# A second Strassen level for one more product of a GEGLU's gate and up stage

## The chip, the cores and the metric

The kernel runs on one core of one Trainium2 chip. The metric is the device time of one execution in microseconds (us); lower is better. A core has TensorE (PE, matrix products into eight PSUM banks), VectorE (DVE), ScalarE (ACT), GpSimd (POOL) and SyncE (SP). The last two serve here mainly to issue DMAs: SP loads from DRAM, POOL stores, loads from buffers in DRAM and DMAs that add onto what is there. Each engine runs its own instructions in program order and waits on semaphores for the others.

## The reference

```python
g = sigmoid((x * gate_w).sum(-1, keepdims=True))
a = dft_seq_re @ (x @ dft_hid_re.T) - dft_seq_im @ (x @ dft_hid_im.T)
b = (gelu(x @ w_gate) * (x @ w_up)) @ w_down
return g * a + (1 - g) * b
```

`x` is 2048 x 640 (S x D), `w_gate` and `w_up` 640 x 1728 and `w_down` 1728 x 640, all in float32; gelu is the tanh form.

## The kernel before

Each float32 factor is held as two parts, a high one in the reduced type fp32r and a low one, the rest. A block product is three matmuls of 128x128 by 128x512 (`mm3`, high x high, high x low, low x high), accumulated in a PSUM bank of 128x512. `high` is a copy by ScalarE that rounds. The low part is made in two ways: `low` is a subtraction by VectorE; `negative` with `left_of` is ScalarE's copy of the raw value with the sign turned, and then an accumulating DMA on POOL's queue that adds to it.

The work runs in stages: the first chunk of gate and up, with x loaded and split (to about 45 us); gate and up for f = 1 to 12, chunks of 128 columns of `w_gate` and of `w_up` (to 337); the product with `w_down` (to 508); the DFT over the sequence; the DFT over the hidden axis, and the mix. All of the stages use Strassen's scheme in the Winograd form, with seven products of half size instead of eight, whose sums and differences VectorE makes.

In gate and up a chunk f is a 2x2 system: the left factors are blocks A11, A12, A21, A22 of the weights and their sums S1 to S4, the right factors B11 to B22 of x and T1 to T4, for each of two halves of the tokens (`tp` 0 and 1). A block is two block products long (index i), and a fifth row block, `g5` and `u5`, goes with it. `gate_up(f, ..., tp, ...)` is a generator that issues these products; at each `yield` the caller decides what comes next. Its banks are X (`pX`) and Z (`pZ`).

`pair_of(f)` gives the kind of a chunk. f = 1 and 2 are kind 0, each by itself. From f = 3 (`PAIRED`) chunks go in pairs, (3,4) to (11,12), the first of a pair of kind 1, the second of kind 2. Over a pair (two chunks) and the two halves of the tokens, the product A12 B21 is a 2x2 system of its own, and `together` computes it with a second Strassen level in seven block products instead of eight, with banks H, Z and V (`pH5t`, ...). Its left factors (`wq`) come from `make_w`, its right factors from `sums_across`, whose parts are kept in DRAM and loaded for each pair anew by `load_across` on POOL's queue (tiles `xq`). Its results are the tiles `s1`, to which the two `gate_up` of each chunk add.

SBUF tiles of 4 KB a partition come from a ring of 47 (`slot`, tag `s4`), tiles of 128x512 from a ring of 12 (`mtile`). A new tile waits until all that read or wrote the tile that had its place are done, DMAs among them.

The order on PE, ScalarE, VectorE and POOL is the order of the program text (`in_order`). Work for coming chunks lies in a queue `fills` of (cost, function) and is taken out in order by `fill` as PE's work goes on, in proportion to `pe_all`. In a chunk this holds: the sums left from the chunk before (`todo`), the left factors of f + 1 (`make_w`), the sums of `w_down` (`sum_wd`) and the totals for the gate g (`load_z`: a load of 128x640, `xz`, by SP, and a product and total by VectorE). In kind 1 these z totals are spread over the queue, three a chunk (four in the last). The results h and their differences are stored to DRAM (`keep`, tiles `hA` and `hT`).

Of the kernel before, what the change touches and what calls it, by code (L numbers as in the profile page):

```python
# [33 lines left out]
def kernel(  # L34
# [93 lines left out]
    wsd = [dram.tile([P, 8, P], F32, tag=f"wsd{k}", name=f"wsd{k}") for k in range(NK)]  # L128
    acc4 = dram.tile([P, 2, T], F32, tag="acc4", name="acc4")
# [21 lines left out]
    def load_x(tp):  # L151


        n = f"{tp}"
        B, r = {}, {}
        src = xt[2 * tp : 2 * tp + 2]

        def tiles(t):
            for k in (1, 2):
                r[k, t] = pair(F32, f"xr{n}{k}{t}")  # L160
                B[k, t] = hl(f"x{n}{k}{t}")
            if t == 1:
# [12 lines left out]
        def tsum(i):  # L175

            a, b = {1: ((1, 2), (1, 1)), 2: ((2, 2), "T1"), 3: ((2, 2), (1, 2)), 4: ((2, 1), "T2")}[i]
            r[f"T{i}"] = pair(F32, f"xs{n}{i}")
            tt(r[f"T{i}"], r[a], r[b], op=ALU.subtract)
            B[f"T{i}"] = hl(f"xT{n}{i}")  # L180

        def his(*keys):
# [22 lines left out]
    def load_w(f):  # L205
# [8 lines left out]
        if pair_of(f) == 1:  # L214
            rq = slot(F32, [P, 8, P], f"wq{f}r")
            nc.sync.dma_start(rq[:, 0:3], wf[f, :, 0:3])
        wraw[f] = ra, rb, rq

    def make_w(f):
# [5 lines left out]
        g23, g5, g01, u23, u5 = ra[:, 0:2], ra[:, 2], ra[:, 3:5], ra[:, 5:7], ra[:, 7]  # L225
# [29 lines left out]
        def diff_here():  # L255
            tt(ra[:, 2], g5, u5, op=ALU.subtract)

        low_from = 2 if kind == 2 else 0

        def high_a():  # L260
            own["a"] = parts("wa")
            high(own["a"][0][:, low_from:], ra[:, low_from:])

        def neg_a():
            negative(own["a"][1][:, low_from:], ra[:, low_from:])

        def low_a():
            a = own["a"]
            left_of(a[1][:, low_from:], ra[:, low_from:])
            W["u5"] = at(a, 7)  # L270
            if kind == 2:
                W["D"] = at(a, 2)
            else:
                W["g5"] = at(a, 2)
            for i in range(2):
                W["A12", i], W["A11", i], W["A22", i] = at(a, i), at(a, 3 + i), at(a, 5 + i)
# [8 lines left out]
        def low_q():  # L285
            q = own["q"]
            left_of(q[1][:, 1:], rq[:, 1:])
# [8 lines left out]
        def neg_c():  # L296
            negative(own["c"][1], own["s"])

        def low_c():
            c = own["c"]  # L300
            left_of(c[1], own["s"])
# [4 lines left out]
        def parts_of(hi, neg, lo):  # L306
            return [(0, hi), (0, neg), (0, lo)]

        a, c = parts_of(high_a, neg_a, low_a), parts_of(high_c, neg_c, low_c)
        if kind == 1:  # L310
            q = parts_of(high_q, neg_q, low_q)
            work = [*a[:2], (84, across), a[2], (56, across2), *q[:2], (84, sums), q[2], (84, sums2), *c[:2], (56, diff), c[2]]
        elif kind == 2:
            work = [(28, diff_here), *a[:2], (84, sums), a[2], (84, sums2), *c]
        else:
            work = [*a[:2], (84, sums), a[2], (84, sums2), *c[:2], (56, diff), c[2]]
# [49 lines left out]
    def together(f, W, Tp, s1, xs):  # L366
# [7 lines left out]
        s1[0, 0] = copy(H, f"s1{f}00")  # L374
# [31 lines left out]
    def gate_up(f, W, B, tp, s5, s1t, xs):  # L406
# [17 lines left out]
        if not kind:  # L424
            s1 = copy(X, f"s1{n}")
# [5 lines left out]
        if not kind:  # L431
            V = bank(f"pV{n}")
            prod(V, "A12", (2, 1), True)
            mm3(V, W["g5"], x1, False, True)
            yield 204
            tt(s1, s1, V, op=ALU.add)
# [5 lines left out]
        if not kind:  # L442
            nc.scalar.activation(s1, s1, AF.Gelu_apprx_tanh)
# [20 lines left out]
        prod(X, "A22", "T4", False)  # L464
        mm3(X, W["u5"], x1, False, True)
        yield 204
        tt(s2, s2, s5, op=ALU.mult)  # L467
        keep(hA[tp][k], 1 + 2 * second, s2)
        tt(s1, s1, X, op=ALU.mult)
# [21 lines left out]
    def sums_left(r, a21, to):  # L491


        a11, a12, a22 = r[:, 0:2], r[:, 2:4], r[:, 6:8]
# [13 lines left out]
    def sum_wd(k):  # L508

        r, a21 = slot(F32, [P, 8, P], f"dr{k}"), wsmall(F32, f"da{k}")  # L510
        nc.sync.dma_start(r, wd[k, :, :8])
        nc.sync.dma_start(a21, wd[k, :, 8:])
        return sums_left(r, a21, wsd[k])

    def sum_wu(p):


        r, a21 = slot(F32, [P, 8, P], f"ur{p}"), wsmall(F32, f"ua{p}")
        nc.sync.dma_start(r, wu[p, :, :8])
        nc.sync.dma_start(a21, wu[p, :, 8:])  # L520
        yield
        if p > 1:
            for a, b in ((0, 2), (2, 4), (4, 5), (5, 8)):
                if p < 4 or a not in (0, 4):
                    nc.scalar.activation(r[:, a:b], r[:, a:b], AF.Copy, scale=-1.0)
            if p < 4:
                nc.scalar.activation(a21, a21, AF.Copy, scale=-1.0)
            nc.gpsimd.dma_start(wneg[p], r)
            yield
        for _, do in sums_left(r, a21, wsu[p]):  # L530
            do()
        yield

    def gate_rows():

        nc.scalar.activation(z, z, AF.Sigmoid)
# [304 lines left out]
    with in_order(ACT, DVE, PE):  # L841
        nc.scalar.activation(table, table, AF.Gelu_apprx_tanh)
        idle = bank("idle")
        for k in range(14):
            nc.tensor.matmul(idle[:, : T // 2], *ones, start=True, stop=True, skip_group_check=True)
# [78 lines left out]
    Tp, t_raw = {}, {}  # L924

    def sums_across():


        raw = {}

        def load(name, b, d):
            raw[name] = mtile(F32, f"xp{name}")
            nc.sync.dma_start(raw[name], xt[b, d])

        for name, b, d in (("11", 0, 2), ("12", 2, 2), ("22", 2, 3), ("21", 0, 3)):
            load(name, b, d)

        def sums():
            raw["t1"] = mtile(F32, "xpt1")
# [7 lines left out]
        def part(k, v, src):  # L947
            return lambda: split(*v, src) or Tp.update({f"T{k}": v})

        def part_out(k, v, src):  # L950
            def do():
                part(k, v, src)()
                for i, p in enumerate(v):
                    nc.gpsimd.dma_start(across_t[k][:, i], p.bitcast(F32))
# [3 lines left out]
        pairs = hl("xpT")  # L958
        Tp.update(B11=at(Bs[0][2, 1], 0), B21=at(Bs[0][2, 1], 1), B22=at(Bs[1][2, 1], 1))

        def part3():
            part_out(3, (mtile(F32R, "xp3h"), mtile(F32R, "xp3l")), raw["12"])()

        def part1():
            part_out(1, at(pairs, 0), raw["t1"])()

        work = [(138, sums), (69, part1), (138, sums2), (69, part_out(2, at(pairs, 1), raw["22"])), (69, part3)]
        return work, [(69, part(4, at(Bs[1][2, 1], 0), raw["21"]))]

    across_t = {k: dram.tile([P, 2, T], F32, tag=f"xp{k}", name=f"xp{k}") for k in (1, 2, 3)}  # L970

    def load_across(f):
        if pair_of(f) != 1 or f == PAIRED:
            return
        for k in (1, 2, 3):
            v = slot(F32R, [P, 2, T], f"xq{f}{k}")
            nc.gpsimd.dma_start(v, across_t[k])
            Tp[f"T{k}"] = v[:, 0], v[:, 1]
# [20 lines left out]
    s1t = {}  # L999
    with in_order(PE, ACT, DVE, POOL):  # L1000
        for f in range(1, NF):
            kind = pair_of(f)
            if f == PAIRED:
                fills.extend(t34)
            fills.extend(todo)
            todo.clear()
            if f == PAIRED - 1:
                t12, t34 = sums_across()
                fills.extend(t12)
            if f + 1 < NF:  # L1010
                nxt, work = make_w(f + 1)
                fills.extend(work)
            if f >= PAIRED and (kind == 1 or f == NF - 1):
                fills.extend(sum_wd((f - PAIRED + 1) // 2))
            if kind == 1:
                more, zs = list(fills), load_z(4 if f > NF - 3 else 3)
# [7 lines left out]
            state.update(pe=0, done=0, all=sum(c for c, _ in fills), pe_all=2450 if not kind else 2790 if kind == 1 else 2040)  # L1024
            s5 = pair(F32, f"s5{f}")
            xs = {}
            work = [gate_up(f, W, Bs[tp], tp, s5[:, tp], s1t, xs) for tp in range(2)]
            more = together(f, W, Tp, s1t, xs) if kind == 1 else iter(())
            for _ in range(4):
                run(more)  # L1030
            for step in range(8 if not kind else 7):
                for tp, w in enumerate(work):
                    run(w)
                    if (step, tp) in ((0, 1), (1, 0)):
                        run(more)
                        if step == 0:
                            run(more)
                if step == 5:
                    load_w(f + 2)
                if step == 4:  # L1040
                    load_across(f + 1)
                if f == NF - 1 and step > 4:
                    load_k(step - 4)
            while fills:
                fills.popleft()[1]()
            if f == NF - 1:
                gate_rows()
            W = nxt
        for _, do in todo:
            do()  # L1050
# [3 lines left out]
    for i in range(len(kseq)):  # L1054
# [14 lines left out]
        step_k(i)  # L1069

# [376 lines left out]
```

## Time and profile before

| | us |
|---|---|
| median of 3 runs | 1026.74 (1025.98 to 1027.36) |
| the profiled execution | 1025.88 |
| its span | 1024.1 |
| VectorE busy | 759.8 |
| ScalarE busy | 475.4 |
| gate and up, f = 5 and 6 (143.2 to 191.5) | 48.3 |

The profile's page gives for each engine the busy time, its share of the span and the number of instructions; the chain that ended last, followed back from the last instruction; and the costliest groups of instructions. The trace can be asked for a stretch of time (windows), for what an engine waited for (waits), for groups of instructions by line, and for DMAs. A row of a group reads: line, engine, operation, out<-in, partitions x elements and type, how many; then the busy time and the mean of one in ns; then the idle time ahead of it and what ended most of it. A DMA row reads: out<-in, the queue, how many, KB each, and the median us from issue to landing. Buffer numbers are left out of names, so `pX` is any chunk's X bank and `s` any result tile.

### The profile page before, as it was taken

Reading aid. Unit: us, or ns where it says so; the run is one execution under the profiler, and the core shown is the slowest. Engines: PE = TensorE matmul, PEld = TensorE weight load, DVE = VectorE, ACT = ScalarE, POOL = GpSimd, SP = SyncE. Lnnn points to the kernel's source line nnn. Section 1 sums busy time; section 2 is a strip of 40 time slices with the busy share of each in tenths; the row PEclk is TensorE's granted clock in tenths of the full one; section 3 lists DMA queues with packets and bytes.
Section 4 is the critical chain, followed back from the end, with each engine's and each line's share of the span. In section 5 each row is a group of like instructions: output and inputs, shape, how many; then the busy total and the mean of one; then the engine's idle time right before and its main releaser. Section 6 shows DMA issues by size and latency. Waiting matters only on the chain.

```text
span 1024.1 us, 13114 instructions
## 1 busy us (share of the span) xinstructions
PE 1019.9 (100%) x4525; PEld 844.5 (82%) x4525; DVE 759.8 (74%) x1067; ACT 475.4 (46%) x609; POOL 186.9 (18%) x317
## 2 busy tenths in 40 slices
PE   9999999999999999999999999999999999999998
PEld 7888888888888888888888888888888888888887
DVE  6966756556566959976898975888488869797794
ACT  5645435353443647555455443444344344355340
POOL 0122433332433200100011012102110200021121
PEclk9999999999999999999999999999999999999999
DMA  7566887979799988968766768657875877997855
GB/s 269 167 183 195 266 251 227 284 187 282 205 310 323 380 295 301 345 184 296 279 209 220 263 235 312 231 193 261 300 245 196 282 265 280 328 314 221 264 142 91
DMA packets 87140, 258.19 MB, mean 252 GB/s; under 512 B 11585, under 2 KB 20961, under 8 KB 87073
## 3 DMA queue, kind: packets, MB, share of 16 engines
q1 hardware_dynamic: 59440, 171.34, 48.9%
q0 software_dynamic: 27344, 85.82, 28.6%
q8 instruction: 35, 0.57, 0.2%
q14 instruction: 33, 0.26, 0.1%
q10 hardware_dynamic: 288, 0.20, 0.1%
HBM read 177.54 MB, written 65.55 MB: 237 GB/s over the span
## 4 chain that ended last, share of the span: by engine, by line
PE 99%; DMA 0%; SPq 0%; DVE 0%; ACT 0%; issue 0%
PE pX L99 8%; PE pX L98 8%; PE pX L97 8%; PE pZ L99 5%; PE pZ L98 5%; PE pZ L97 5%; PE pL L98 3%; PE pL L99 3%; PE pL L97 3%; PE pV L98 2%; PE pV L99 2%; PE pV L97 2%; PE pY L98 1%; PE pR L98 1%; PE pQ L98 1%; PE pY L99 1%
## 5 line engine op out<-in xcount | busy, mean ns | idle before, releaser
L78 ACT ACTIVATE ch<-csa 128x1024 fp32r<-128x1024 f32 x32 | 34.0, 1063 | 88.3 <-DVE csa L612 73.4
L81 DVE TENSOR_TENSOR cl<-cra,ch 128x1024 fp32r<-128x1024 f32 x32 | 39.1, 1223 | 29.9 <-ACT ch L78 14.6
L457 DVE TENSOR_TENSOR s<-s,pX 128x512 f32<-128x512 f32 x24 | 16.5, 687 | 56.1 <-PE pX L99 41.7
L78 ACT ACTIVATE ch<-cra 128x1024 fp32r<-128x1024 f32 x32 | 33.9, 1058 | 51.1 <-PE pL L98 25.3
L98 PE MATMUL pL<-cl,xah 128*128 128x512 f32 x128 | 49.8, 389 | 0.0
L99 PE MATMUL pL<-ch,xal 128*128 128x512 f32 x128 | 49.8, 389 | 0.0
L97 PE MATMUL pL<-ch,xah 128*128 128x512 f32 x128 | 49.3, 389 | 0.0
L441 ACT ACTIVATE s<-pZ 128x512 f32<-128x512 f32 x24 | 14.4, 598 | 69.1 <-PE pZ L99 47.5
L81 DVE TENSOR_TENSOR cl<-crb,ch 128x1024 fp32r<-128x1024 f32 x32 | 39.1, 1222 | 8.1 <-ACT ch L78 7.2
L78 ACT ACTIVATE ch<-crb 128x1024 fp32r<-128x1024 f32 x32 | 33.8, 1055 | 19.9 <-DVE cl L81 8.2
L81 DVE TENSOR_TENSOR cl<-csb,ch 128x1024 fp32r<-128x1024 f32 x32 | 39.2, 1225 | 4.0 <-ACT ch L78 2.3
L81 DVE TENSOR_TENSOR cl<-csa,ch 128x1024 fp32r<-128x1024 f32 x32 | 39.0, 1219 | 3.6 <-DMA wsu<-ur 3.6
L81 DVE TENSOR_TENSOR kl<-kw,kh 128x1024 fp32r<-128x1024 f32 (+1 forms) x26 | 31.4, 1209 | 13.3 <-ACT kh L78 13.3
L78 ACT ACTIVATE ch<-csb 128x1024 fp32r<-128x1024 f32 x32 | 34.0, 1063 | 10.5 <-DVE csb L615 7.0
L143 ACT ACTIVATE s<-pX 128x512 f32<-128x512 f32 x44 | 25.6, 595 | 24.2 <-PE pX L99 23.8
L746 POOL DMA_DIRECT2D out<-ks x12 | 6.5, 543 | 163.8 <-DVE ks L745 163.2
L1116 POOL DMA_DIRECT2D uA<-c x8 | 4.3, 544 | 166.8 <-DVE c L1204 166.6
L342 POOL DMA_DIRECT2D hA<-s x48 | 26.4, 549 | 34.7 <-DVE s L467 25.0
L342 POOL DMA_DIRECT2D hT<-s x48 | 26.1, 544 | 27.0 <-DMA hA<-s 7.2
L78 ACT ACTIVATE kh<-kw 128x1024 fp32r<-128x1024 f32 (+1 forms) x26 | 27.1, 1042 | 7.7 <-issue 3.5
L462 ACT ACTIVATE s<-s 128x512 f32<-128x512 f32 x24 | 14.9, 629 | 33.7 <-DVE s L461 33.7
L97 PEld LDWEIGHTS pL<-ch,xah 128*128 128x128 f32 x128 | 24.0, 188 | 5.0
(3680 smaller groups left out, 3445.6 us busy)
## 6 DMA issues: line engine op xcount, KB each, us to landing
cra<-in_ct SPq DMA_DIRECT2D x64, 512.0 KB, 4.1
crb<-in_ct SPq DMA_DIRECT2D x64, 512.0 KB, 5.0
hA<-s POOLq DMA_DIRECT2D x48, 256.0 KB, 6.4
hT<-s POOLq DMA_DIRECT2D x48, 256.0 KB, 6.1
kr<-hA SPq DMA_DIRECT2D x24, 512.0 KB, 8.3
kr<-hT SPq DMA_DIRECT2D x24, 512.0 KB, 6.8
ux<-uA SPq DMA_DIRECT2D x24, 512.0 KB, 6.1
ux<-uT SPq DMA_DIRECT2D x16, 512.0 KB, 6.5
```

What stands on the lines that cost most here:

```text
L78: nc.scalar.activation(hi, raw, AF.Copy)
L81: nc.vector.tensor_tensor(lo, raw, hi.bitcast(F32), op=ALU.subtract)
L97: nc.tensor.matmul(ps, lh, rh, start=first, stop=False, skip_group_check=True)
L98: nc.tensor.matmul(ps, lh, rl, start=False, stop=False, skip_group_check=True)
L99: nc.tensor.matmul(ps, ll, rh, start=False, stop=last, skip_group_check=True)
L143: nc.scalar.activation(m, src, AF.Copy)
L342: nc.gpsimd.dma_start(to[:, i], src)
L441: nc.scalar.activation(s5, Z, AF.Copy)
L457: tt(s5, s5, X, op=ALU.add)
L462: nc.scalar.activation(s2, s2, AF.Gelu_apprx_tanh)
L746: nc.gpsimd.dma_start(acc4[:, t] if tp and e == 4 else out[2 * tp + t, e], src)
L1116: nc.gpsimd.dma_start(to[:, i], src)
```

## The change

The product A22 T4 is given the second level too. In before each `gate_up` of a pair's chunks computes it with two block products, eight for the pair. In after a new generator `together_up` does it once for the pair, with seven, on banks `pH5u`, `pZ5u`, `pV5u`. Its parts:

- Right factors. T4 of both halves is written to DRAM (`t4d`). `sums_across` now serves both systems; it makes T1 to T3 of T4's 2x2 system (`xv`), keeps them in DRAM, and `load_across` loads them in f = 5, 7, 9 and 11 (tiles `xu`) after the first and the second step of the chunk's two `gate_up`. T4's own fourth sum takes the place of a block of T4 in SBUF.
- Left factors. `load_up` loads raw blocks of both chunks of `w_up` (tile `wu`), `make_up` makes four sums and the high and low parts.
- Results. Four tiles `s4`, onto which each `gate_up` adds its own bank X; then it multiplies as before. The product with `u5` stays in `gate_up`.
- PSUM. Where bank H and bank V both need the product P1 (in `together` and `together_up`; in kind 0 banks X and V), ScalarE copies H to V, and PE accumulates further products onto what is there (`start=False`); the result is then copied out of V. In before ScalarE copied H to SBUF and VectorE added V. The matmuls at the start of the kernel, which compute nothing that is used, now write both halves of a bank.
- Low parts. `left_of` is replaced by `low` on VectorE, but for `wa` and `wq` of kind 1 with f > 3.
- Order. In a chunk of kind 1 come first `todo`, then `make_up`, then the sums of `w_down`, with four z totals spread among these (from f = 5), and behind them `make_w(f + 1)`. The loads for the sums of `w_down` are issued at the head of the chunk. For the last chunk the sigmoid and `gate_rows` come earlier, and its `todo` after the first step of the product with `w_down`.
- Sizes. The ring of slots has 46 tiles instead of 47, that of 128x512 tiles 14 instead of 12; `sum_wu` uses the small ones. The host lays out the chunk's weights `wf` in another order.

```diff
-        return pool.tile(shape, dt, tag="s4", name=name, bufs=47)
+        return pool.tile(shape, dt, tag="s4", name=name, bufs=46)
-        return pool.tile([P, T], dt, tag="m", name=name, bufs=12)
+        return pool.tile([P, T], dt, tag="m", name=name, bufs=14)
...
+    def load_up(f):
+        r = slot(F32, [P, 8, P], f"wu{f}r")
+        nc.sync.dma_start(r[:, 0:2], wf[f, :, 2:4])
+        nc.sync.dma_start(r[:, 6:8], wf[f - 1, :, 2:4])
+        return r
+    def make_up(f, r):
+        W, own = {}, {}
+        def across():
+            tt(r[:, 2], r[:, 0], r[:, 1], op=ALU.add)
+            tt(r[:, 4], r[:, 6], r[:, 0], op=ALU.subtract)
+            tt(r[:, 3], r[:, 2], r[:, 6], op=ALU.subtract)
+            tt(r[:, 5], r[:, 7], r[:, 3], op=ALU.subtract)
+        def high_u():
+            own["u"] = [slot(F32R, [P, 8, P], f"wu{f}{n}") for n in "hl"]
+            high(own["u"][0][:, 1:6], r[:, 1:6])
+        def low_u():
+            u = own["u"]
+            low(u[0][:, 1:6], u[1][:, 1:6], r[:, 1:6])
...
+        return W, [(112, across), (0, high_u), (78, low_u)]
...
+            if kind == 1 and f > PAIRED:
+                left_of(a[1], ra)
+            else:
+                low(*a, ra)
...
-            left_of(c[1], own["s"])
+            low(*c, own["s"])
...
         mm3(H, W["A12", 0], Tp["B11"], True, True)
         yield 68
-        s1[0, 0] = copy(H, f"s1{f}00")
+        nc.scalar.activation(V, H, AF.Copy)
...
-        mm3(V, W["A12", 1], Tp["B21"], True, False)
+        mm3(V, W["A12", 1], Tp["B21"], False, False)
         mm3(V, W["g5"], x1[0], False, True)
         yield 136
-        tt(s1[0, 0], s1[0, 0], V, op=ALU.add)
+        s1[0, 0] = copy(V, f"s1{f}00")
...
+    def together_up(f, W, Wp, s4):
+        H, Z, V = (bank(f"p{name}{f}u") for name in "HZV")
+        (b11, b21), (_, b22) = ([at(Bs[tp]["T4"], i) for i in range(2)] for tp in range(2))
+        mm3(H, W["A22", 0], b11, True, True)
+        yield 68
+        nc.scalar.activation(V, H, AF.Copy)
+        yield
+        mm3(Z, Wp["S1p"], Tu["T1"], True, True)
+        yield 68
+        s4[1, 1] = copy(Z, f"s4{f}11")
+        yield
+        mm3(V, W["A22", 1], b21, False, True)
+        yield 68
+        s4[0, 0] = copy(V, f"s4{f}00")
+        yield
+        mm3(H, Wp["S2p"], Tu["T2"], False, True)
+        yield 68
+        s4[0, 1] = copy(H, f"s4{f}01")
+        yield
+        mm3(H, Wp["S3p"], Tu["T3"], False, True)
+        yield 68
+        tt(s4[1, 1], s4[1, 1], H, op=ALU.add)
+        yield
+        mm3(Z, Wp["S4p"], b22, False, True)
+        yield 68
+        tt(s4[0, 1], s4[0, 1], Z, op=ALU.add)
+        yield
+        mm3(H, Wp["A22p"], Tu["T4"], False, True)
+        yield 68
+        s4[1, 0] = copy(H, f"s4{f}10")
+        yield
...
-        prod(X, "A22", "T4", False)
+        if not kind:
+            prod(X, "A22", "T4", False)
         mm3(X, W["u5"], x1, False, True)
...
-        tt(s1, s1, X, op=ALU.mult)
+        if kind:
+            c21 = s4[kind - 1, tp]
+            tt(c21, c21, X, op=ALU.add)
+            tt(s1, s1, c21, op=ALU.mult)
+        else:
+            tt(s1, s1, X, op=ALU.mult)
...
+    def load_across(f, n, to, kept, k):
+        v = slot(F32R, [P, 2, T], f"{n}{f}{k}")
+        nc.gpsimd.dma_start(v, kept[k - 1])
+        to[f"T{k}"] = v[:, 0], v[:, 1]
...
+            if kind == 1:
+                up, work = make_up(f, load_up(f))
+                fills.extend(work)
+            if kind == 1:
+                lw, *w = sum_wd((f - PAIRED) // 2)
+                lw[1]()
+                fills.extend(w)
...
                 nxt, work = make_w(f + 1)
-                fills.extend(work)
...
+                if kind != 1 or f == PAIRED:
+                    fills.extend(work)
+            if kind == 1 and f > PAIRED:
+                more, zs = list(fills), load_z(4)
                 fills.clear()
                 for k, v in enumerate(zs):
                     a, b = (len(more) * i // len(zs) for i in (k, k + 1))
                     fills.extend(more[a:b] + v)
+                fills.extend(work)
...
+                    if (2, 0) < (step, tp) < (6, 0):
+                        run(more_up)
+                if step < 2 and kind == 1 and f > PAIRED:
+                    for k in ((1,), (2, 3))[step]:
+                        load_across(f, "xu", Tu, keptu, k)
+                if step == 4 and pair_of(f + 1) == 1 and f + 1 > PAIRED:
+                    for k in (1, 2, 3):
+                        load_across(f + 1, "xq", Tp, keptp, k)
```

More of the change, by code (lines that the diff above doesn't have):

```diff
@@ L128 @@
     wsd = [dram.tile([P, 8, P], F32, tag=f"wsd{k}", name=f"wsd{k}") for k in range(NK)]
+    t4d = [dram.tile([P, 2, T], F32, tag=f"t4{p}", name=f"t4{p}") for p in range(2)]
     acc4 = dram.tile([P, 2, T], F32, tag="acc4", name="acc4")
@@ L424, in gate_up @@
         if not kind:
-            s1 = copy(X, f"s1{n}")
+            V = bank(f"pV{n}")
+            nc.scalar.activation(V, X, AF.Copy)
         else:
@@ L844 @@
         for k in range(14):
-            nc.tensor.matmul(idle[:, : T // 2], *ones, start=True, stop=True, skip_group_check=True)
+            nc.tensor.matmul(idle[:, halves[k % 2]], *ones, start=k == 0, stop=True, skip_group_check=True)
         bk1, bk2 = first_banks(0, 1), first_banks(0, 2)
@@ L1069 @@
         step_k(i)
+        while todo:
+            todo.popleft()[1]()
     ukw, uraw, uks, ukb = {}, {}, {}, {}
```

205 lines of the change are left out of this document (114 added, 91 removed).

## The prediction

> **What bounds the kernel now.** I read the page first: busy shares, the clock and the chain that ended last.
>
> ```profile
> PE 1019.9 (100%) x4525; PEld 844.5 (82%) x4525; DVE 759.8 (74%) x1067; ACT 475.4 (46%) x609; POOL 186.9 (18%) x317
> ...
> PEclk9999999999999999999999999999999999999999
> ...
> PE 99%; DMA 0%; SPq 0%; DVE 0%; ACT 0%; issue 0%
> ```
>
> TensorE (PE) is busy for 1019.9 of 1024.1 us at full clock, and 99% of the last chain lies on it. The view of waits, for PE alone, says whether it ever stands:
>
> ```profile
> PE idle L845 <- PEq L1435: 0.8, 1, 0.8
> ```
>
> Once, before the first matmul. So the time is the number of matmuls times their spacing, and a wait costs only what it opens as a gap on PE. The windows give the spacing and what the others do in the stage changed (columns: us; PE, PEld, DVE, ACT, POOL busy with counts; clock; DMA share; GB/s):
>
> ```profile
> 143.20:171.10 27.90, 27.90 (x124) 23.08 (x123) 19.43 (x38) 12.42 (x19) 10.63 (x19) 1.00 0.87 257
> 171.10:191.50 20.40, 20.40 (x91) 16.89 (x90) 9.03 (x22) 8.26 (x13) 6.49 (x10) 1.00 0.81 227
> 508.00:900.00 392.00, 392.00 (x1731) 324.59 (x1730) 311.59 (x390) 172.06 (x202) 48.17 (x89) 1.00 0.74 255
> ```
>
> The third row is a long stretch of one kind of matmul: 392.00 / 1731 = 0.2265 us each. The first two are one pair, f = 5 and 6. Gate and up hold five pairs, (3,4) to (11,12). Within a pair VectorE (DVE) is busy 28.5 of 48.3 us and ScalarE (ACT) 20.7: neither bounds. The DMA engines, at 0.87 and 0.81, are the nearest to full, and at the head of a pair they are full:
>
> ```profile
> 143.20:147.00 3.80, 3.80 (x18) 3.18 (x17) 3.77 (x8) 1.30 (x3) 2.76 (x5) 1.00 1.03 177
> 147.00:151.00 4.00, 4.00 (x19) 3.30 (x19) 3.13 (x6) 0.60 (x1) 1.08 (x2) 1.00 0.97 362
> 151.00:155.00 4.00, 4.00 (x20) 3.30 (x19) 2.95 (x6) 0.60 (x1) 1.63 (x3) 1.00 1.03 418
> ```
>
> **The change, part by part.** (1) Matmuls. In a pair A22 T4 was 8 block products of 3 matmuls; it becomes 7. That is 3 fewer of 213, five times: 15 x 0.2265 = 3.40 us saved. These lie on PE, so they count in full if PE stays without gaps.
>
> (2) VectorE and ScalarE, by these groups (mean ns after the comma):
>
> ```profile
> L143 ACT ACTIVATE s<-pX 128x512 f32<-128x512 f32 x20 | 12.0, 598 | 3.9 <-PE pX L99 3.7
> L462 ACT ACTIVATE s<-s 128x512 f32<-128x512 f32 x20 | 12.4, 629 | 29.0 <-DVE s L461 29.0
> L89 ACT ACTIVATE wa6l<-wa6r 128x768 fp32r<-128x768 f32 x1 | 0.8, 838 | 0.0
> L89 ACT ACTIVATE ws6l<-ws6r 128x1024 fp32r<-128x1024 f32 x1 | 1.0, 1049 | 0.0
> L469 DVE TENSOR_TENSOR s<-s,pX 128x512 f32<-128x512 f32 x20 | 13.7, 686 | 3.2 <-PE pX L99 3.1
> L81 DVE TENSOR_TENSOR kl<-kw,kh 128x1024 fp32r<-128x1024 f32 x1 | 1.2, 1227 | 2.1 <-ACT kh L78 2.1
> L564 DVE CUSTOM_DVE_ANT_0 xz<-xz,gwb 128x640 f32<-128x640 f32 x15 | 12.3, 820 | 3.5 <-DMA xz<-in_xz 3.5
> ```
>
> VectorE in a pair gains six 128x512 adds (two in the new product, four of c21) less the one that the seeded bank saves, 5 x 0.69 = 3.4; two 128x1024 low parts and one of 128x512 in place of accumulating DMAs, 3.1; the four small sums and the low part of the new left factors, about 1.2 + 0.8; one more z total, 0.9. That is +9.4 on 28.5, so 37.9 of 47.6. ScalarE gains six copies (3.6) and the high part of wu (0.7) and loses three negations (2.9) and a third of a high part (0.2): +1.2 on 20.7. A copy that writes PSUM rather than SBUF has no row; I bound it by 0.60 and 0.63, the rows that read PSUM and SBUF, and take 0.60. All this lies beside 47.6 us of PE and costs nothing by its sum, only by its order. For f = 1 and 2 the seeded V bank leaves PE some 0.5 us between the copy and its use by these rows; I put nothing there, 0.5 for each of the four at worst.
>
> (3) DMA. A pair loses three accumulating DMAs (384, 512, 512 KB) and gains three loads of 512 KB (xu1 to xu3), two of 128 KB (wu) and a z load: about as many bytes as before. Writing T4 and its sums out, once, and the moved loads of wd and wu come to nothing where PE does not wait for them.
>
> (4) The order of waits, which is where I expect the time to go. The left factors wu and the right factors xu are made and loaded inside the kernel of f = 5, 7, 9 or 11 that uses them, and their slots come from a ring of 46 that stores and loads of the previous pair still hold. Reading the built program's waits on each engine, f = 5 gives one chain. Times count from its first matmul; PE needs a thing at (matmuls ahead of it) x 0.2265.
>
> - xz0, the first z load, takes a slot that PE's 6th matmul still reads (factor xq1): issued at +1.5.
> - VectorE has its z total first in its queue. The stores' differences hT, two 128x512 subtractions, stand behind it.
> - The second difference goes out by POOL's queue; ScalarE's high part wuh takes a slot which that store must have read.
> - VectorE's low part wul follows wuh.
> - xu2 is loaded by POOL's queue into the slot of the raw wu, which wul must have read. POOL's queue is held meanwhile: xu3 and the stores of wd's sums stand behind.
> - PE needs xu2 at its 97th matmul: 96 x 0.2265 = 21.7.
>
> Transfers, from issue to landing, where before has them at the same place of a pair (last column), and over all pairs:
>
> ```profile
> xz<-in_xz SPq DMA_DIRECT2D x1, 320.0 KB, 7.9
> xz<-in_xz SPq DMA_DIRECT2D x1, 320.0 KB, 8.0
> xz<-in_xz SPq DMA_DIRECT2D x1, 320.0 KB, 8.6
> ...
> hT<-s POOLq DMA_DIRECT2D x2, 256.0 KB, 4.7
> hT<-s POOLq DMA_DIRECT2D x34, 256.0 KB, 5.9
> ...
> xq<-xp POOLq DMA_DIRECT2D x2, 512.0 KB, 7.2
> xq<-xp POOLq DMA_DIRECT2D x2, 512.0 KB, 6.6
> ...
> DMA to landing us min/median/max: 2.8/6.5/9.1
> ```
>
> The last row is of all 13 z loads. xu has no row of its own; xq is the same tile and queue. The 128x640 high and low parts have none either: ScalarE's lies between 0.60 (128x512) and 0.84 (128x768), I take 0.73; VectorE's between 0.69 (128x512) and 1.23 (128x1024), I take 0.82. Two adds back to back start 0.60 apart in the timeline (148.83, 149.44):
>
> ```profile
> 148.83 0.69 DVE L429 TENSOR_TENSOR s<-s,pX 128x512 f32<-128x512 f32 x1
> 149.44 0.69 DVE L485 TENSOR_TENSOR s<-s,s 128x512 f32<-128x512 f32 x1
> ...
> 153.63 0.82 DVE L564 CUSTOM_DVE_ANT_0 xz<-xz,gwb 128x640 f32<-128x640 f32 x1
> ```
>
> The sum: 1.5 + 8.0 (xz0) + 0.9 (z total) + 1.3 (two differences) = 11.7; + 4.7 (store) = 16.4; + 0.73 + 0.82 = 17.95; + 6.6 (xu2) = 24.5. PE stands from 21.7 to 24.5: **2.8 us**. In before the z total at the head of f = 5 ran at 153.63, 10.4 after the pair's start, and nobody waited for it; here four steps of a chain stand behind it. What is late next is ScalarE: wuh holds back the copies behind it, and the seed of the new V bank, which PE needs at its 88th matmul (19.7), comes up to 1 us late; that gap is part of the 2.8, since it moves the need for xu2 as well. For f = 7, 9 and 11 the slots fall the same way. The pair (3,4) has no z sums, and I find its slack near 0. So 4 x 2.8 = 11.2.
>
> Bounds of one stall: with the shortest z load (2.8) it is gone; with 6.5, 4.7 and 6.6 it is 1.3; with 8.6, 5.9 and 7.2 it is 5.2.
>
> The profiled execution took 1025.88 us, 0.86 under the median of 1026.74: 1025.88 - 3.40 + 11.2 = 1033.7, and with the 0.86, **1034.5**.
>
> A rule that speaks against a gap: the Trainium skill, "TensorE: Matmul & The Clock Gate", section "What's actually happening", has PE's clock fall to half after an idle window of about 3.4 us and take about as long to come back. The trace agrees that there are two rates, with these rows:
>
> ```profile
> 0.78 3.15 PE L845 MATMUL idle<-const-bfloat16-1.0 128*128 128x256 bf16 x14 [0.78 <-PEq L1435]
> ...
> 1017.07 0.28 PE L97 MATMUL yLlast<-ub190h,uw04h 128*128 128x256 f32 x1
> 1017.19 0.28 PE L98 MATMUL yLlast<-ub190l,uw04h 128*128 128x256 f32 x1
> ```
>
> 256 columns go every 0.21 us at the start and every 0.12 at the end. By that rule a stall in one piece would cost about 1.7 us more, 6.8 over four pairs; mine is below the window and comes in pieces, so the sum goes without it.
>
> **The rivals.** *Gapless.* The three landings need only sum to 16.5 instead of 19.3 for PE never to wait. For it: the change takes accumulating DMAs off POOL's queue, and the z load's median is 6.5, not 8. Against it: the engines were full at 143 to 155, and f = 5 now loads 1.8 MB more there. Then -3.40 stands alone: 1023.3.
>
> *A ring.* A stall in f = 5 delays VectorE's queue, where the next kernel's left factors now stand behind wul, the sums of wd and the fourth z. By the row sums VectorE then runs twenty instructions without a break from about +26 to +40.5 before ScalarE can split wq of f = 7 (two instructions of 0.95); wq's accumulating DMA goes out at about +43 and xq2, whose slot it must have read, follows it. Such DMAs landed in
>
> ```profile
> wq7l<-wq7r POOLq DMA_DIRECT2D x1, 448.0 KB, 4.9
> ...
> ws7l<-ws7r POOLq DMA_DIRECT2D x1, 512.0 KB, 7.2
> ```
>
> PE needs xq2 at 225 x 0.2265 = 51.0. With 4.9 and 6.6 it lands at 54.5, 3.5 late, of which PE has lost 2.8 already; with 7.2 and 7.2 at 57.4, 6.4 late. Its middle, 5.0 per pair, gives 4 x 5.0 - 3.4 = +16.6: 1043.3. For it: the work behind the z sums is the longest in VectorE's queue. Against it: it takes the longer landings twice over.
>
> *Not what it says:* stalls of 0.6 to 1.0 us that cancel the saving, 1026 to 1028.5.
>
> **How the numbers follow.** Forecast, stalls of 1.3 to 4.2 per pair, 1028.5 to 1040: 0.50. Ring, over 1040: 0.15. Gapless, or less than 0.3 per pair: 0.28. Cancelled: 0.07. Two tenths of a per cent, 2.05 us, is what a measurement of this kernel can tell from no change (its three runs lie 1.4 apart). Gapless is faster by 3.4, so faster 0.28; same 0.07; slower 0.65. The range takes in gapless and the ring's middle: 1022.8 to 1044; the likeliest case's own is 1028.5 to 1040.
>
> **What would show it.** PE waits, none now, on the second transfer xu in f = 5, 7, 9 and 11, of 2 to 4 us, and windows around 20 to 26 us into each pair with PE below full; matmul records fewer by 15; first z total some 10 us into a pair and the store behind it landing at about +16. I am wrong if the waits list stays empty, if the landings sum below 16.5, if PE waits more in the second kernels of pairs or in f = 1 and 2, or if the clock falls.

## The result, and the profile after

The changed kernel takes 1029.26 us (median of 12 runs, 1027.87 to 1031.19) beside 1026.17 of the kernel before (12 runs): a ratio of 1.0028 (95% interval 1.0019 to 1.0037), so 3.1 us slower. The profiled execution took 1028.01, 2.13 more than that of before (1025.88). All times here are of executions with a mean granted clock of 0.98 or more; two executions of one kernel below, 1129 and 1276 us at 0.85 and 0.75, are left out.

The page of the changed kernel, busy time and chain by engine:

```profile
PE 1019.4 (99%) x4510; PEld 840.5 (82%) x4510; DVE 809.0 (79%) x1142; ACT 477.4 (47%) x629; POOL 179.5 (17%) x319
...
PE 92%; DMA 3%; DVE 2%; issue 2%; ACT 1%; POOL 0%; DVEq 0%; POOLq 0%; ACTq 0%; SPq 0%
```

The 15 matmuls are gone, but the chain leaves PE for 8% of the span: DMA, VectorE, ScalarE. The view of PE's waits, where before had the first start alone (us in total, times, longest):

```profile
PE pH9u L97 <- DMA xu<-xv: 1.1, 1, 1.1
PE idle L941 <- PEq L1551: 0.8, 1, 0.8
PE pH11t L97 <- DVE s L437: 0.6, 1, 0.6
PE pH5t L97 <- DVE s L437: 0.4, 1, 0.4
PE pH7t L97 <- DVE s L437: 0.3, 1, 0.3
```

That is 2.4 us beside the start, and less than what PE lost, because the recorded end of a matmul (0.39 us after its start) covers the first 0.16 of each gap. The timeline of PE shows it:

```profile
154.96 0.39 PE L99 MATMUL pZ<-x15h,wa5l 128*128 128x512 f32 x1
155.76 0.50 PE L97 MATMUL pH5t<-x121h,wq5h 128*128 128x512 f32 x1 [0.41 <-DVE s L437]
156.09 0.40 PE L98 MATMUL pH5t<-x121l,wq5h 128*128 128x512 f32 x1
```

From start to start it is 0.80 and 0.33 instead of 0.23 twice, so this gap cost 0.57 + 0.11. Summed in that way over all starts, the gaps of gate and up come to 5.4 us: 2.4 at this place (bank H of the first product, PE's 58th matmul of a pair), 0.7 at bank V of the second, 0.7 at xu1, 1.6 at xu2 (the first and second transfer `xu` of a pair). And -3.40 + 5.4 = +2.0, where the two profiles differ by 2.13. The first matmuls of f = 5, 7, 9 and 11 give the same by pair, before and then after:

```profile
143.19 0.39 PE L97 MATMUL pH5t<-x021h,wa5h 128*128 128x512 f32 x1
...
191.52 0.39 PE L97 MATMUL pH7t<-x021h,wa7h 128*128 128x512 f32 x1
...
239.84 0.39 PE L97 MATMUL pH9t<-x021h,wa9h 128*128 128x512 f32 x1
...
288.17 0.39 PE L97 MATMUL pH11t<-x021h,wa11h 128*128 128x512 f32 x1
```

```profile
142.26 0.39 PE L97 MATMUL pH5t<-x021h,wa5h 128*128 128x512 f32 x1
...
191.00 0.39 PE L97 MATMUL pH7t<-x021h,wa7h 128*128 128x512 f32 x1
...
239.94 0.39 PE L97 MATMUL pH9t<-x021h,wa9h 128*128 128x512 f32 x1
...
289.70 0.39 PE L97 MATMUL pH11t<-x021h,wa11h 128*128 128x512 f32 x1
```

A pair took 48.33 before. After, f = 5 starts 0.93 earlier, 0.33 of it ahead of f = 1 and 0.60 in the pair (3,4), which has three matmuls fewer, and then the pairs take 48.74, 48.94 and 49.76 where 210 matmuls without a gap need 47.6.

Where this begins is seen on VectorE at the head of f = 5 (its timeline after; the pair starts at 142.26):

```profile
151.86 0.83 DVE L660 CUSTOM_DVE_ANT_0 xz<-xz,gwb 128x640 f32<-128x640 f32 x1 [4.28 <-DMA xz<-in_xz]
152.61 0.08 DVE L660 DVE_READ_ACCUMULATOR2_ANT z<- 128x1 f32 x1
152.61 0.69 DVE L562 TENSOR_TENSOR s<-s,s 128x512 f32<-128x512 f32 x1
153.22 0.69 DVE L564 TENSOR_TENSOR s<-s,s 128x512 f32<-128x512 f32 x1
153.82 0.68 DVE L508 TENSOR_TENSOR s<-s,pX 128x512 f32<-128x512 f32 x1
154.42 0.69 DVE L568 TENSOR_TENSOR s<-s,s 128x512 f32<-128x512 f32 x1
155.02 0.68 DVE L437 TENSOR_TENSOR s<-s,pH5t 128x512 f32<-128x512 f32 x1
```

VectorE stands 4.28 us for the z load. Then it does the z total (both rows of L660) and what has piled up behind: three differences of the pair before (L562, L564, L568), an addition (L508), and only as the fifth behind the total the addition of bank H (L437), for which PE stands until 155.76.

### The profile page after: what moved, and what is told of

Read it like the earlier page. It is cut to its first block, busy times and chain, and to the rows that moved or that the text cites. A ratio compares the mean times of both kernels' runs of the same rounds, so it can differ in the third digit from the quotient of the medians.

```text
span 1026.2 us, 13230 instructions
## 1 busy us (share of the span) xinstructions
PE 1019.4 (99%) x4510; PEld 840.5 (82%) x4510; DVE 809.0 (79%) x1142; ACT 477.4 (47%) x629; POOL 179.5 (17%) x319
## 3 DMA queue, kind: packets, MB, share of 16 engines
q0 software_dynamic: 26864, 84.45, 25.4%
## 4 chain that ended last, share of the span: by engine, by line
PE 92%; DMA 3%; DVE 2%; issue 2%; ACT 1%; POOL 0%; DVEq 0%; POOLq 0%; ACTq 0%; SPq 0%
PE pX L99 6%; PE pX L98 6%; PE pX L97 6%; PE pZ L99 4%; PE pZ L98 4%; PE pZ L97 4%; PE pL L99 3%; PE pL L98 3%; PE pL L97 3%; DMA xz<-in_xz 2%; PE pV L99 2%; PE pV L98 2%; PE pV L97 2%; PE pY L99 1%; PE pY L98 1%
## 5 line engine op out<-in xcount | busy, mean ns | idle before, releaser
L81 DVE TENSOR_TENSOR cl<-cra,ch 128x1024 fp32r<-128x1024 f32 x32 | 39.1, 1223 | 22.9 <-ACT ch L78 22.7
L144 ACT ACTIVATE s<-pX 128x512 f32<-128x512 f32 x40 | 23.3, 594 | 10.6 <-PE pX L99 10.3
L98 PEld LDWEIGHTS pL<-cl,xah 128*128 128x128 f32 x128 | 24.0, 188 | 5.0
```

Source lines behind the costliest of these rows:

```text
L81: nc.vector.tensor_tensor(lo, raw, hi.bitcast(F32), op=ALU.subtract)
L98: nc.tensor.matmul(ps, lh, rl, start=False, stop=False, skip_group_check=True)
L144: nc.scalar.activation(m, src, AF.Copy)
```

## The experiments

Four theories were put to the test. A time such as +9.5 counts from the pair's first matmul; wuh and wul are the high and low part of the tile `wu`; square brackets behind a ratio to the kernel before hold its 95% interval. A: VectorE's queue at the head of a pair, behind the first z total. B: the seed, ScalarE's copy of H to V. C: the streamed factors on GpSimd's queue. D, formed after the first four runs: what a tile must wait for in its slot, and what stands behind the instruction that waits.

**z totals behind the next chunk's left factors.**

```diff
...
-                for k, v in enumerate(zs):
-                    a, b = (len(more) * i // len(zs) for i in (k, k + 1))
-                    fills.extend(more[a:b] + v)
                 fills.extend(work)
+                for v in load_z(4):
+                    fills.extend(v)
```

> The changed kernel with its four z totals (and their loads) behind the next chunk's left factors in the queue of f = 5, 7, 9 and 11, nothing else. Theory A (VectorE, in order, stands at the head of a pair until the first z load has landed, about +9.5, and everything behind it is late): the gaps of 2.4 us at H of the first product, 0.7 at V, 0.7 and 1.6 at xu1 and xu2 all go; PE gaps under 1 us in all, time 1023 to 1024, 3 under the kernel before. Theory B (the seed: ScalarE must copy H to V while PE waits): the 0.7 at V stays and the time is about 1024.5. Theory C (streaming: the right factors come late over POOL's queue and a full ring of slots whatever VectorE does): 2 to 3 us stay, 1026 or more.

1043.27 us, 1.0160 [1.0146, 1.0174], where A had 1023 to 1024. PE's waits, the three largest:

```profile
PE pV7u L97 <- ACT pV7u L457: 4.5, 1, 4.5
PE pV9u L97 <- ACT pV9u L457: 4.3, 1, 4.3
PE pV5u L97 <- ACT pV5u L457: 4.0, 1, 4.0
```

All waits at H are gone, as A has it, and wuh ran at 150.86 instead of 158.74. But the sum I made of that was far off. By its time the run would fit C (1026 or more), but PE stood at V and not at xu. ScalarE's timeline has the new wait:

```profile
161.77 0.63 ACT L78 ACTIVATE wa<-wa6r 128x512 fp32r<-128x512 f32 x1 [4.69 <-DMA wsd<-dr]
...
165.25 0.59 ACT L457 ACTIVATE pV5u<-pH5u 128x512 f32<-128x512 f32 x1
```

Without z tiles in between, the ring gives the high part of the next chunk's wa the slot of the raw `w_down` blocks, whose stores stand behind xu1's load in GpSimd's queue. ScalarE waits 4.69 us, and the seed of V stands six instructions behind. The order of allocation, not the amount of work, made this wait: theory D.

**z totals between the sums of w_down and the next chunk's factors.** The same edit with `fills.extend(work)` last.

> The changed kernel with its four z totals after the sums of w_down and ahead of the next chunk's left factors. Theory A: as in the first run, since the head of the pair is free of z here too: 1023 to 1024.5. If what counts is the amount of VectorE's work ahead of the next chunk (a ring, as I had it for a rival), the next chunk's factors come late and PE waits 0.5 to 2 us in f = 6, 8, 10 and 12: 1025 to 1031.

1053.74 us, 1.0264 [1.0250, 1.0278]. No wait at H; 3.5 to 5.3 us a pair at the copy of H ahead of xu3's product, and 0.2 to 1.5 at xu. The copy stands in ScalarE's queue behind the high part of the next chunk's wa, and that waits for VectorE, where the z totals and the waits for their loads now stand ahead:

```profile
168.66 0.63 ACT L78 ACTIVATE wa<-wa6r 128x512 fp32r<-128x512 f32 x1 [5.77 <-DVE wa6r L292]
```

Both expectations were too low. The waits lie in f = 5, 7, 9 and 11, not in the second chunks, so it is not the ring of late factors either.

**Bank V not seeded.**

```diff
-        nc.scalar.activation(V, H, AF.Copy)
+        s4[0, 0] = copy(H, f"s4{f}00")
...
-        mm3(V, W["A22", 1], b21, False, True)
+        mm3(V, W["A22", 1], b21, True, True)
...
-        s4[0, 0] = copy(V, f"s4{f}00")
+        tt(s4[0, 0], s4[0, 0], V, op=ALU.add)
```

and the same in the first product.

> The changed kernel with bank V of the two pair products not seeded: ScalarE copies H to SBUF and VectorE adds V, as in the kernel before, in both products. Theory B: the gap at V (0.35 for each pair, in two of them) and what it moves go, 1026.5 to 1028. Theory A: VectorE has two more additions of 0.69 in a queue that is late, so the gap at H of the first product grows by up to 0.6 for each pair: 1029 to 1032.

1038.84 us, 1.0121 [1.0107, 1.0135]. The waits at H in f = 5 and 11 rose from 0.4 and 0.6 to 0.9 and 1.2, as A expected (in f = 7 and 9 they were 0.2); but in f = 5, 7 and 9 waits of 2.0 to 2.7 at the copy of H ahead of xu3's product were new, and the time is above either expectation. VectorE now stood for a later z load as well, with ScalarE's copies behind it:

```profile
167.19 0.83 DVE L660 CUSTOM_DVE_ANT_0 xz<-xz,gwb 128x640 f32<-128x640 f32 x1 [3.57 <-DMA xz<-in_xz]
```

So taking the seed away did not bring the time back, as B has it. It is no pure test of the seed, since two tiles are also taken from their ring earlier; which of the two made the new waits is not shown.

**The kernel before with z first.** In before's queue, `make_w(f + 1)` goes behind the rest and four z totals are spread over that rest, as in the change.

> The kernel before with one part of the change alone: four z totals spread among the queue's head, the next chunk's left factors behind them. Theory A says that the head of a pair is what costs, so some gap at H of the first product shows here too, 0.2 to 0.7 for each pair: 1027 to 1029. Theories B and C: no gap, 1026.2, since neither a second seed nor streamed factors are in it.

1058.67 us, 1.0321 [1.0303, 1.0340]. PE's waits:

```profile
PE pZ L99 <- DMA ws12l<-ws12r: 7.6, 1, 7.6
PE pH7t L97 <- DVE s L392: 2.9, 1, 2.9
PE pH9t L97 <- DVE s L392: 2.8, 1, 2.8
PE pH5t L97 <- DVE s L392: 2.5, 1, 2.5
```

The wait at H appears in a kernel with neither a second seed nor streamed factors, 1.5 to 2.9 us a pair against 0.3 to 0.6 in the changed kernel: A's place and cause, shown. The size was missed twice: at H, where 0.2 to 0.7 was expected, and in all, since the accumulating DMAs of the next chunk's `ws` now also come late (7.6, and 2.2 in each of three other pairs). The change's `low` on VectorE in place of these DMAs is then what lets it live with this order at all; that reading is from these waits alone, and no run undid `low` in the changed kernel.

**z loads where they are, totals one place later.**

The two parts of `load_z` are taken apart, as `load` and `total`.

```diff
...
-                    fills.extend(more[a:b] + v)
+                    fills.extend(more[a:b])
+                    if k:
+                        fills.append(total)
+                    if k < 3:
+                        fills.append(load)
+                fills.append(total)
```

> The changed kernel with its z loads issued where they are, but each z total one place further back in the queue: the first after all the stores' differences of the pair before, the second after the four sums of wu, the last two after the sums of w_down. So the ring of slots gives out the same order of tiles but for xu. Theory A: the first total still runs at about +9.5, but nothing of the pair before stands behind it; the gaps at H of the first product (2.4 us in all) go, wuh starts at +13 to +14 instead of +16.4, and the gaps at V, xu1 and xu2 (3.0 in all) go with it: PE gaps under 0.8 us, 1023 to 1024, 2.2 to 3.2 under the kernel before. Theory D, from the first four runs (what decides is which slot ScalarE's copies for the next chunk get, since they stand ahead of the seed of V in its queue): a gap at V or at the copies of the second product opens as in those runs, 2 us or more a pair: 1034 or more.

1037.67 us, 1.0104 [1.0087, 1.0121]. No wait at H, as A has it, but its time was missed:

```profile
PE pH11u L97 <- DMA xu<-xv: 3.7, 1, 3.7
PE pH7u L97 <- DMA xu<-xv: 2.4, 1, 2.4
```

The costs in the queue had moved too, so the sums of `w_down` were issued ahead of xu2's load, and their four stores stood ahead of it on GpSimd's queue: it went out at 162.99 instead of 160.78 in f = 5. The time is in D's range; of the gap that D expected at V there were 0.6 to 0.9 us in three pairs, and most stood at xu2.

**xu by SyncE's queue.**

```diff
-        nc.gpsimd.dma_start(v, kept[k - 1])
+        if n == "xu":
+            nc.sync.dma_start(v.bitcast(F32), kept[k - 1])
+        else:
+            nc.gpsimd.dma_start(v, kept[k - 1])
```

> The changed kernel with the loads of xu issued by SyncE's queue instead of GpSimd's, in the same places. Theory C (POOL's queue makes the streamed factors late): the gaps at xu1 and xu2 go, 2.3 us, and the rest stays: 1026 to 1027. Theory A: xu2's load still waits for wul, which waits for the z totals, so the gaps at H stay (2.4) and those at xu stay within 1 us of what they were: 1028 to 1030; 1 to 3 more if the third z load holds them back in SyncE's queue.

1048.15 us, 1.0206 [1.0177, 1.0234]. The waits at xu grew (2.6 in f = 9, 1.2 in f = 7) and those in ScalarE's queue came on top (1.4 to 2.1), so the time is above both expectations. In f = 5 xu1 landed at +15.9 instead of +18.0. But the stores ahead of wuh now took 6.2 us instead of 2.9, wuh started at +18.2 instead of +16.5, and xu2 went out at +19.8 and landed at +25.4 instead of +22.2: its slot held it back, not GpSimd's queue. Since the stores changed as well, this alone does not settle theory C; it falls with the last run, where xu goes by GpSimd's queue and the view of waits has none for it.

**The third total ahead of the sums of w_down.** As the run with later totals, with the pieces of the queue cut so that one z total more is done before the sums of `w_down`.

```diff
...
+                for k, (a, b) in enumerate(((0, 2), (2, 4), (4, 6), (6, 7), (7, 9))):
+                    fills.extend(more[a:b])
+                    if k:
+                        fills.append(total)
+                    if k < 3:
+                        fills.append(load)
```

> As the run with later z totals, but the third total stays ahead of the sums of w_down, so that these come behind the loads of xu again in GpSimd's queue, as in the changed kernel; and the ring now gives xu2 a slot that only PE's 63rd matmul still reads (+14), xu3 the slot of the raw wu. Theory A with this order: no gap at H of the first product, xu2 landed by +20 and not waited for; a gap at V of 0.6 to 0.8 in three pairs stays, since wuh still waits for the store and stands ahead of eight copies: PE gaps 2 to 2.5 us, time 1025 to 1026.2. Theory C or D: 2 us a pair at xu, 1034 or more.

1025.47 us (11 runs), 0.9992 [0.9983, 1.0000], as A expected: 3.8 less than the changed kernel, by order alone, with the same work. PE's waits beside the starts:

```profile
PE pV5u L97 <- ACT pV5u L457: 0.8, 1, 0.8
PE pH11u L97 <- ACT s L144: 0.8, 1, 0.8
```

xu2 now gets a slot that is free at +14 and lands at +19.1 to +20.0; PE comes for it at +21.8 to +22.9.

**wuh one place later.** An empty entry ahead of it in the queue.

> The run above with ScalarE's high part of wu one place later in its queue, behind the first copy of Z, and with it in the ring. If the gap at V comes from wuh waiting for a store with the other copies behind it, taking one copy (0.5 us) from behind it makes that gap 0 to 0.5 smaller where the store lands no later: 1024.5 to 1026. If the store that wuh now waits for lands later by what the copy saved, nothing changes.

1027.56 us, 1.0014 [1.0003, 1.0024], 2.1 more. The slot that wuh now gets waits for the next store, landed at +16.5 in f = 5 instead of +15.8, and the waits at V were 1.0, 0.8 and 0.3. Worse than either expectation: the copy saved was less than the store's delay, and a wait of 0.5 opened in f = 3 and one of 0.8 at H in f = 11.

**GELUs behind the seed, with the good order.**

```diff
-        if kind:
-            s1 = s1t[kind - 1, tp]
-            nc.scalar.activation(s1, s1, AF.Gelu_apprx_tanh)
         yield
         mm3(Z, W["D"], x2, False, False)
         yield 68
+        if kind:
+            s1 = s1t[kind - 1, tp]
+            nc.scalar.activation(s1, s1, AF.Gelu_apprx_tanh)
```

> The run with later z totals and xu ahead of the sums of w_down, and besides the two GELUs of the pair's first results after the product with D instead of ahead of it, so behind the copy of H to V in ScalarE's queue. Theory A: the gap at V is ScalarE's queue behind wuh; with two instructions of 0.5 us less ahead of the copy the gaps there (1.05 and 0.33 in the profile of the run without this) go: PE gaps 1 to 2 us, 1023.5 to 1024.8. If the gap is wuh's alone, whatever stands behind it, the time stays at 1025.5.

1025.27 us, 0.9991 [0.9982, 1.0000]. The waits at V are gone, but at the next copy of H, behind ScalarE's high part of ws (1.05 us), PE now waits 0.7 in f = 5 and 7 too, beside the 0.8 in f = 11 that the run without this edit had. The saving moved on instead of coming out.

**GELUs behind the seed, in the changed kernel.** The same edit alone.

> The changed kernel with the two GELUs moved in that way and nothing else. Theory A: the gap at V (0.7 in all) goes, those at H of the first product (2.4) and at xu (2.3) stay, xu2's up to 0.7 larger since V's gap no longer covers it: 1028 to 1029.2, a quarter or less of what the order of the z totals gave. If the seed's copy were the cause of the stalls, the time would come back to 1024.5 to 1026.

1028.26 us (median of 6 executions), 1.0023 [1.0012, 1.0034]. V's waits are gone and the time does not come back: against B, and in the range of A. The other places did not stay as A expected, though. By the starts the gaps at H grew from 2.4 to 3.3 us, and those at xu fell from 2.3 to 1.0. The first z load says why (landing counted from the pair's first matmul, gap at H by the starts):

| | f = 5 | f = 7 | f = 9 | f = 11 |
|---|---|---|---|---|
| changed kernel, landed | 9.43 | 9.32 | 9.04 | 9.61 |
| changed kernel, gap at H | 0.68 | 0.57 | 0.29 | 0.86 |
| this run, landed | 10.48 | 8.20 | 7.80 | 10.35 |
| this run, gap at H | 1.72 | 0 | 0 | 1.59 |

In all eight the gap is the landing less 8.75 us, to 0.01, and nothing where the load landed before that: the gap at H is the first z load's, as A has it. A larger gap at H also leaves xu2 more time to land, so the two change against each other.

**The high part of ws two places later.** In the run with the good order and later GELUs:

```diff
-            work = [(84, sums), (28, diff_here), (0, high_a), (84, sums2), (0, high_c), ...
+            work = [(84, sums), (28, diff_here), (0, high_a), (84, sums2), (0, lambda: None), (0, lambda: None), (0, high_c), ...
```

> The run with later z totals and later GELUs, and besides ScalarE's high part of the next chunk's sums (ws, 128x1024, 1.05 us) two places further back in the queue, behind the copy of H that frees it for xu3's product. In the profile of the run without this the three gaps left in gate and up (0.9 to 1.0 each, 3.0 in all) stood at that copy. If theory A and what follows from it hold (a wait is that of ScalarE's or VectorE's queue, and order alone decides it), they go: PE gaps in gate and up under 0.5 us, 1022.8 to 1024, 2.3 to 3.5 under the kernel before, which is the 3.4 of the matmuls saved. If the next chunk's factors are then late, a gap opens in f = 6, 8, 10 and 12 instead: 1025 or more.

1022.97 us (7 runs), 0.9977 [0.9966, 0.9988] beside 1025.74 of before, as expected: 2.8 faster than before. The page and the waits of this kernel:

```profile
PE 1017.0 (100%) x4510; PEld 841.6 (82%) x4510; DVE 808.0 (79%) x1142; ACT 478.0 (47%) x629; POOL 179.5 (18%) x319
```

```profile
PE idle L941 <- PEq L1555: 0.8, 1, 0.8
```

In this view PE stands nowhere but at the start, with the changed kernel's counts of instructions and with both seeds and xu where they were (by the starts, small gaps of 0.45 us in all are left in f = 11 and 12). Its pairs:

```profile
142.32 0.39 PE L97 MATMUL pH5t<-x021h,wa5h 128*128 128x512 f32 x1
...
190.02 0.39 PE L97 MATMUL pH7t<-x021h,wa7h 128*128 128x512 f32 x1
...
237.70 0.39 PE L97 MATMUL pH9t<-x021h,wa9h 128*128 128x512 f32 x1
```

47.70 and 47.68, against 48.33 of before: 0.65 less a pair for three matmuls (0.68 by the spacing).

## Why the prediction was right in direction and wrong in size

The forecast was 1034.5, 7.8 slower than before; measured is 3.1 slower. The matmuls were worth about what was said (last run: 0.65 a pair for 0.68). The cover of all else by PE's 47.6 us was right: a pair took 37.0 us of VectorE (37.9 forecast) and 21.3 of ScalarE (21.9), the copies into PSUM took 0.58 to 0.62 (0.60 taken), and f = 1 to 4 had no gap. The bytes, "about as many", were not the same: in f = 5 and 6 the windows have 266 GB/s over 48.74 us, against 244 over 48.30 before, 1.2 MB more.

The chain at the head of the pair was right in its places, and up to the second difference almost to the tenth. Times from the pair's first matmul:

| step | forecast | f = 5 | f = 7 | f = 9 | f = 11 |
|---|---|---|---|---|---|
| xz0 issued | 1.5 | 1.6 | 1.6 | 1.6 | 1.6 |
| xz0 landed | 9.5 | 9.4 | 9.3 | 9.0 | 9.6 |
| second difference done | 11.7 | 11.6 | 11.5 | 11.2 | 11.8 |
| store landed | 16.4 | 14.9 | 15.1 | 14.4 | 15.3 |
| wuh starts | 16.4 | 16.5 | 16.4 | 16.1 | 16.7 |
| wul done | 17.95 | 18.1 | 18.0 | 17.7 | 18.3 |
| xu2 landed | 24.5 | 22.2 | 22.8 | 23.7 | 21.4 |

That the slots fall the same way in f = 11, as the prediction had it, is wrong. There xu2 went out before wul began, into a slot for which a store had to be done:

```profile
306.86 0.55 POOL L1066 DMA_DIRECT2D xu<-xv  x1 [2.60 <-DMA hT<-s]
...
307.16 0.82 DVE L81 TENSOR_TENSOR wu11l<-wu11r,wu11h 128x640 fp32r<-128x640 f32 x1
```

What failed first is the term "6.6 (xu2)". I took the landing of xq, the same tile on the same queue. xu2 in f = 5, 7, 9 and 11 took:

```profile
xu<-xv POOLq DMA_DIRECT2D x1, 512.0 KB, 3.7
...
xu<-xv POOLq DMA_DIRECT2D x1, 512.0 KB, 4.4
...
xu<-xv POOLq DMA_DIRECT2D x1, 512.0 KB, 5.6
...
xu<-xv POOLq DMA_DIRECT2D x1, 512.0 KB, 4.2
```

On average 4.5, 2.1 less. So only f = 9, with 5.6, waits for xu2 for long (1.4; f = 7 0.2); the gaps at V, xu1 and xu2 come to 0.75 a pair, where I had 2.8.

The trace of before had the better row. For each pair three xq are loaded. The rows that I took are of the first two, which go out 0.6 us apart and right behind the accumulating DMA of wq. The third goes out some 4 us later, and for f = 5 and 7 it took:

```profile
xq<-xp POOLq DMA_DIRECT2D x1, 512.0 KB, 4.6
...
xq<-xp POOLq DMA_DIRECT2D x1, 512.0 KB, 3.8
```

For f = 9 and 11 it is 3.8 and 4.5: the size of xu2. Why the first two take longer stays open; no run tests it. The shares of the DMA engines do not explain it: they were 1.03 and 0.86 in the stretches of the first two xq, and 0.75, 0.90, 0.79 and 1.10 in those of the four xu2, where the load at 1.10 landed in 4.2 and the one at 0.79 in 5.6.

The store was shorter as well, 2.7 to 3.2 from issue to landing for 4.7. The three landings (xz0, store, xu2) therefore sum to 14.4, 15.3, 15.8 and 15.4, all under the 16.5 that I had named as a sign of being wrong. That PE still waited at xu2 in f = 7 and 9 comes of steps that the sum did not have: the true wait of wuh, below, and 0.4 us from the end of wul to xu2's issue.

The second failure is an omission on the other side. I followed the z total to the store and to wuh, but not to the addition of bank H, fifth behind it in VectorE's queue, for which PE stands 39 matmuls before xu2: 0.6 a pair that the sum did not have. Together 0.75 + 0.60 = 1.35 a pair, 5.4 in all, against 11.2. The two parts are not independent, since a gap leaves what stands behind it time to land. An estimate from the landings in the table: without the gap at H, PE would have come to xu2 at 21.7 and stood 0.5, 1.1, 2.0 and 0 us there, 3.6 of the 5.4.

A smaller point is the reason for wuh's start. I had the store; it landed 1.1 to 2.0 earlier than forecast, and wuh started when the four sums of wu were done, which stand behind the second z total on the same VectorE:

```profile
158.74 0.74 ACT L78 ACTIVATE wu5h<-wu5r 128x640 fp32r<-128x640 f32 x1 [1.53 <-DVE wu5r L240]
```

The right time came of the wrong wait.

Of the rivals, the gapless case is what the last run reached with another order; the changed kernel is not it. The ring did not occur: PE had no wait in f = 6, 8, 10 or 12. The profiled run (1028.01) lies in the case where stalls cancel the saving (1026 to 1028.5), and the median just inside the forecast's own range, which began at 1028.5: the stalls were at the low end of what I allowed. That it fell inside is in part luck: the stall at xu2 was far too large, and a gap at H that the sum did not have made up for some of it.

## What to carry to other kernels

A change that saves matmuls on a full TensorE pays only if every other queue keeps its order of need. Here 15 matmuls were worth 3 us, and the gaps, which began with one early wait (a 320 KB load whose total stood ahead of other work on an in-order engine), took 5.4; three changes of order that change no work gave nearly all of it back.

In a ring of shared slots, moving one allocation changes what every later tile waits for. Such an edit is checked by listing, for each tile needed soon, the last reader of its slot and the queue in which that reader stands; counting busy time does not show it (six of the runs were 11 to 32 us slower than the kernel before, with nearly the same work).

Follow a late instruction to all that stands behind it on its engine, up to the first thing that the bounding engine asks for, not only along the chain that one has in mind.

## What the runs showed of the hardware

TensorE's clock fell after gaps, at a price beside the gap itself. In the run with the z totals last, the windows around the wait of 4.0 us at V:

```profile
166.00:170.00 4.00, 4.00 (x10) 3.14 (x11) 1.18 (x4) 0.96 (x2) 0.00 (x0) 0.50 0.53 169
...
172.00:178.00 6.00, 6.00 (x28) 4.81 (x27) 3.63 (x8) 0.65 (x2) 0.00 (x0) 1.00 0.74 240
```

Ten matmuls in 4 us at a clock of 0.50, then the full rate. Twelve in a row went 0.43 apart instead of 0.23, some 2.5 us in all, so a stall of 4 us cost over 6. Shorter gaps did it too, but not always: by the starts, after 2.2 us (run without the seed, f = 5) eight matmuls were slow, after 2.6 and 2.8 (the same run, f = 7 and 9) none. The Trainium skill, "TensorE: Matmul & The Clock Gate", section "What's actually happening", puts the fall after an idle window of about 3.4 us; half rate and the length of some 3.4 to 5 us agree, but in these runs a gap of 2.2 us was enough. In the changed kernel three of the twelve executions had a mean clock of 0.998, and they are the three longest (1030.50 to 1031.19), though none of the gaps in its profile is over 1.4 us; where in those runs the clock fell is not recorded.
